# Linear attention into a routed MoE: q transposed as it was loaded, Exp and max on one PSUM bank each, another order of loads

## The chip, the cores and the metric

One core of a Trainium2 chip runs the whole program. The metric is the device time of one execution in microseconds, as the median of several runs. The engines are TensorE (PE, with its weight loads as PEld), VectorE (DVE), ScalarE (ACT), GpSimd (POOL) and SyncE (SP). Loads that change the type on the way (fp32 in memory, fp16 on the chip) are issued by POOL, which puts them all in one queue (q0 in the profile); SP issues plain copies in another (q1).

## The reference

```python
def phi(x):
    return np.where(x > 0, x, np.exp(x) - 1.0) + 1.0
q_p, k_p = (phi(q), phi(k))                      # 8 batches, 8 heads, 576 tokens, 64 wide
kv  = np.einsum('bhsd,bhse->bhde', k_p, v)
z   = np.sum(k_p, axis=2)
num = np.einsum('bhsd,bhde->bhse', q_p, kv)
den = np.einsum('bhsd,bhd->bhs', q_p, z)[..., None] + 1e-06
x   = (num / den)                                # -> (4608, 512)
P = np.exp(x @ w_gate - max)                     # 8 experts
for _ in range(8):                               # Sinkhorn
    P /= P.sum(1, keepdims=True) + 1e-09
    P /= P.sum(0, keepdims=True) + 1e-09
    P *= N / E
for e in range(E):                               # w1: 512 x 1024, w2: 1024 x 512
    out += P[:, e:e + 1] * (np.maximum(x @ w1[e], 0.0) @ w2[e])
```

phi is computed as min(exp(x), max(x + 1, 1)), which is the same function: one Exp on ACT, one add-and-max on DVE, one min on DVE.

## The kernel before

The program has two parts that overlap. The **front** (about the first 125 us) is the attention. It goes in 16 steps, `att(b, g)`, one for each batch and each half of the heads; the text calls them step 0 to step 15 (n = 2b + g). While the steps go on, PE already does the first two matrix products of expert 0 for those groups of 512 tokens whose attention is complete: `layer1` (x times w1 into the banks `hq`, line L717) and a plain second layer (h times w2 into `ye`, L1017). Group 0 needs steps 0 and 1 and expert 0's w1, then its w2; group 1 needs steps 0 to 3 as well; and so on. After the front come the remaining groups of expert 0 and the seven other experts, in a Strassen-like form (L832, L1133).

Order of work. Nothing is scheduled by a compiler. A planner written in the kernel (`_Plan`) holds every task with an engine, a cost in microseconds, dependencies, the pools of buffers it takes, and due times (`after`); it emits tasks in the order of its own list schedule. For the front that order is not searched at build time: the string `_FRONT` lists task numbers with a letter for the engine, some 2200 of them, and the planner follows it. Every engine then executes its own list strictly in that order, so one task that waits holds all behind it on the same engine.

What an attention step does, by the lines of the profile:

- Three loads of 576 KB in memory each: k stays fp32 (`kin`), v and q become fp16 (`vv`, and a slice of `hb` for q). In step 0, k and q are both loaded as fp32 by SP; all other loads are POOL's (L406), which waits where the buffer (3 for k, 3 for v, 3 for q) or one of 8 slots in its queue is not free yet.
- k: Exp (`ek`, L417), add-and-max (`t`, L421), min (L425). kv and z: 36 small matmuls (`kv_ps`, L446), copied to `kvz` by ACT (L359) or DVE (L361).
- q: Exp (`eq`, L477) and add-and-max (`tq`, L480) from the loaded tile in SBUF, min (L484), then 36 transposes on PE (L469) into the two PSUM banks of `att`, then one copy to SBUF (`qpT`, L361 on DVE, L359 on ACT).
- Two halves of 288 columns: den matmuls into both `att` banks (L504), Ln (`rden`, L516), then one Exp for both halves (L521) which gives 1/den; num matmuls into `num_ps`, which shares the one pair of banks of `kv_ps` (L504), and the product with 1/den into xT (L531).

The banks of `att` serve the transposes, both den halves and the routing logits (L548), so these follow one another. Before real work is ready PE runs matmuls on zeros (`yw`, L621), 46 of them. Expert 0's w1 comes in two pieces of 512 columns, w2 in two pieces (L335). A step's v can be loaded only when the step three places before it in that buffer has done its kv matmuls. A tiny POOL copy (`gate`, L437) waits for the last step's v to land.

`sinkhorn` (eight rounds on DVE with a tiny matmul in each) runs after the last logits, beside the second part of expert 0.

Of the kernel before, what the change touches and what calls it, by code (L numbers as in the profile page):

```python
# [141 lines left out]
1n 2p 3p 4p 5p 48s 49m 6p 7p 8p 0g 9p 10p 11p 12p 13p 14p 15p 16p 17p 18p 19p 20p 21p  # L142
22p 23p 54a 50s 51m 60n 61a 114g 115m 120a 24p 25p 55d 56d 62d 63d 26p 27p 52g 53m 64p 65d 57n 58p
121d 59a 28p 29p 75g 76m 77g 78m 82d 122d 30p 31p 66p 32p 33p 79g 80m 34p 116g 117m 35p 36p 37p 38p
39p 81a 87n 83d 89d 84n 67a 68p 40p 88a 90d 69a 70a 41p 85p 86d 91p 92d 42p 43p 73p 93p 44p 45p
74d 71p 126n 128d 104n 127a 118g 119m 94a 105g 106m 72d 46p 95p 96a 47p 129d 97a 123n 109n 124p 125d 130p 143g
144m 153n 579n 154a 131d 98p 99d 580p 141g 142m 581p 132p 133a 147a 100p 101d 582p 583p 584p 586p 588p 587a 148d 155d
585a 590p 107g 108m 145g 146m 134p 135a 589d 156d 149d 150n 592p 593a 594p 136a 170g 171m 180n 151p 152a 110g 111m 112g
113m 157p 158d 596p 139p 591a 140d 182d 159p 595a 160a 181a 598p 183d 168g 169m 172g 173m 137p 138d 161p 162a 597a 599a
197g 198m 195g 196m 175d 600p 602p 184p 185d 603p 610a 174a 176d 207n 616n 177n 601p 608a 163a 606p 607p 199g 200m 224g  # L150
225m 226g 227m 178p 179a 186p 187a 166p 167d 201a 208a 604p 236n 164p 209d 165d 202d 203d 210d 204n 188p 605p 617p 618a
619p 620d 621p 189a 190a 622a 211p 238d 253g 254m 212d 205p 230a 206a 228g 229m 251g 252m 280g 281m 102g 103m 282g 283m
231d 623p 625p 624d 626d 213p 193p 194d 237a 239d 232d 214a 627p 614a 628a 629p 215p 216a 217a 191p 192d 631p 649n 632a
233n 612d 240p 241d 234p 235a 255g 256m 637p 218p 242p 243a 635p 244p 630d 258d 257a 245a 219d 220p 259d 260n 284g 285m
263n 265d 221d 292n 334g 335m 293a 264a 287d 638p 636p 222p 643a 223a 650p 651a 652p 266d 645d 267p 246a 653a 311g 312m
309g 310m 307g 308m 261p 268d 314d 262d 286a 654p 656p 657a 655d 294d 319n 336g 337m 633p 269p 295d 249p 250d 658p 660p
659d 288d 321d 320a 270a 313a 639p 661a 247p 271p 272a 273a 315d 248d 662p 289n 340a 663a 296p 297d 290p 291d 322d 640p
361g 362m 338g 339m 274p 298p 275d 299a 365g 366m 634p 535d 300p 301a 276p 277d 367a 664p 536d 665d 316n 682n 317p 323p
318a 647a 302a 341d 363g 364m 392g 393m 390g 391m 542d 368d 324d 683p 684a 685p 342d 686a 346n 348d 347a 668p 278p 279a
373n 374a 543d 375d 687p 688a 303p 444g 445m 325p 326a 369d 537d 304d 689p 453s 376d 544d 349d 690a 641a 669p 305p 327p  # L160
328a 329a 691p 306d 343n 350p 692d 351d 344p 345a 446g 447m 454s 476g 477m 402n 396a 666p 330p 394g 395m 417g 418m 352p
353a 448g 449m 455s 404d 667p 397d 354p 403a 355a 331d 332p 474g 475m 483s 674a 356a 484s 370n 693p 333d 371p 372d 377p
378d 459n 405d 478g 479m 485s 419g 420m 695p 359p 379p 694a 538s 539m 360d 676d 398d 424d 461d 696a 380a 423a 460a 670p
671p 672p 357p 381p 382a 673p 697p 486g 358d 425d 462d 480a 406p 407d 698d 715n 399n 400p 429n 383a 680a 401a 481d 716p
717a 421g 422m 386p 408p 409a 545s 546m 431d 387d 718p 720p 719a 563d 564d 565d 566s 567m 430a 432d 410p 411a 384p 385d
678a 426n 482d 705p 547s 548m 706p 713a 721a 412a 433p 434d 427p 428d 549d 722p 435p 413p 724p 414d 436a 723a 550d 725d
437p 438a 439a 415p 416d 726p 463p 464a 556d 440p 557d 551d 540s 541m 490n 491a 552s 553m 492d 441d 451d 493d 558d 559s
560m 570g 554s 555m 487n 571n 572g 573m 574g 575m 701p 702p 388p 488p 450a 452d 389a 489a 494p 442p 443d 728p 709d 729d
456n 457p 495a 496p 497a 458d 703p 498p 499a 500a 501p 704p 727d 465p 466a 502d 711d 730p 731a 734p 467p 468a 469a 503p
504d 759d 760d 735p 742a 699p 472p 473d 700p 470p 471d 533n 755d 748d 981s 982m 983s 984m 749d 808d 750d 756d 561s 562m  # L170
707a 751s 752m 985s 986m 987s 988m 757d 758d 753s 754m 738p 739p 732p 763n 733p 534p 809d 810d 761d 811s 812m 813s 814m
989s 990m 991s 992m 505p 506a 740a 508d 507n 576n 577g 578m 764p 778p 765a 766p 767a 780p 781a 770p 771a 768p 769a 772p
736p 774p 993s 994m 779a 784p 785a 782p 783a 746a 773d 775d 509p 510d 786p 787d 788p 789d 776p 737p 973d 815n 777a 816p
817a 511d 790p 791a 818p 819a 822p 820p 744d 762d 821a 823a 830p 832p 833a 831a 824p 825d 794p 826p 866d 867d 827d 834p
836p 837a 838p 795p 840p 974d 868d 839d 869s 870m 828p 829a 512p 835a 841d 513d 802d 792p 793p 874p 875a 800a 876p 877a
1023s 1024m 1025s 1026m 568s 569m 1027s 1028m 842p 880p 798p 514d 924d 878p 843a 844d 881a 975d 925d 845d 926d 846d 515p 796p
799p 797p 804a 871s 872m 927s 928m 516d 929s 930m 873n 884p 882p 885d 883d 888p 848p 517d 879a 889a 894p 976d 886p 895a
849a 890p 891a 806a 898p 892p 893a 847d 899d 854p 887a 896p 518p 850p 851a 855a 519d 520d 897d 852p 900p 932p 901a 853a
858p 859d 856p 857d 946p 933a 938p 902d 903d 904d 939a 521p 934p 522d 860p 935a 861a 936p 942p 906p 948p 931n 937a 943d
947a 944p 952p 949a 940p 953a 523d 941d 908p 954p 955d 945a 950p 956p 907a 951a 995p 996a 909a 957d 524p 525d 526d 997p  # L180
958p 998a 1001p 1002a 912p 1003p 1004d 999p 1005p 1006d 959a 913a 916p 917d 910p 527p 905d 528d 529d 1007p 1009p 1011p 1000a 1010a
1012a 918p 1015p 1016a 1008a 1017p 1013p 1014a 1018d 1019p 919a 530p 531d 532d 712a 1020d 1037p 914p 1039p 1038a 613a 972n 1029s 1030m
1031s 1032m 1033s 1034m 1035s 1036m 1485n 1040a 977d 915d 960p 1021p 1043p 1119s 1120m 1121s 1122m 1123s 1124m 1486g 1487m 1488g 1489m 961p
968d 978d 1044a 1022a 1093d 962p 963p 969a 964p 864a 1045p 966p 1094d 979d 1041p 1095d 1046d 1042a 609a 1047p 611d 681a 965p 1048d
1049p 675d 1051p 1053p 648a 1052a 615d 980d 1054a 1050a 967p 1057p 1058a 1059p 1055p 1061p 1065p 1067p 1096d 971d 1062d 1060d 970d 1063p
1056a 1066a 1071p 1068a 911d 1073p 1069p 1097p 1099p 1100d 679d 1064a 1072a 1101d 1098a 1102p 1103a 1075p 1107p 1110p 1076d 1077p 1079p 1108d
1070a 743d 1111d 1109d 646a 1081p 1113p 1078a 1080a 1085p 1125s 1126m 1127s 1128m 1082a 1087p 1086a 1105a 714a 1104g 1106g 1129s 1130m 1083p
1074d 1089p 1133p 1135p 1084a 1114d 1112d 1088d 1115d 1116p 1090d 1091p 1131s 1132m 1241s 1242m 1243s 1244m 1245s 1246m 1490n 1491g 1492m 1134a
1139p 1136a 642a 1092a 1141p 1140a 1137p 1118d 1117d 1161d 1162d 1165p 1167p 1166a 1170p 1143p 1175p 1138a 644a 1163d 1164d 1169d 710d 1168d
1173a 1174g 1171a 1144d 1178p 1145p 1146a 1147p 1177d 1176d 708d 1172g 1148a 1149p 1150a 1181p 1153p 1179d 1142d 1154a 1155p 1151p 1157p 1183d  # L190
1180d 1182d 1158d 1187p 677a 1189p 1184p 1159p 1215d 1216d 1186d 747d 1185d 1217d 741d 1218d 1152a 1188a 1193p 801a 1190a 1195p 1191p 1219p
1221p 1194a 1222d 1196d 1223d 1192a 1220a 1224p 1227a 1228g 923a 1160a 1197p 1198d 1156d 1229p 1231d 1232p 1230d 1493d 865d 1233d 1199p 1200a
1201p 1202a 1203p 1204a 803a 1235p 1207p 1209p 1247s 1248m 1205p 1208a 1211p 1225a 1236d 1494d 1495d 1237d 1249s 1250m 1251s 1252m 1253s 1254m
1255p 1363s 1364m 1365s 1366m 1257p 1238p 1212d 1206a 1256a 1210d 1213p 1261p 1258a 1263p 1259p 1367s 1368m 1214a 807a 1240d 1234d 1239d 1287p
1262a 1288a 1283d 1289p 1292p 1284d 1285d 1293a 1291d 1290d 1286d 1265p 1297p 1300p 745d 1266d 1267p 1260a 1299d 1302d 1298d 1301d 1269p 1271p
1303p 1268a 1270a 1275p 1264d 1272a 1277p 1273p 1304d 1337d 1305d 1276a 1279p 1309p 1311p 1306p 1338d 1274a 1226g 1280d 1281p 1295a 1310a 863a
# [41 lines left out]
def kernel(  # L238
# [17 lines left out]
    P = 128  # L256
# [1092 lines left out]
```

## Time and profile before

| | us |
|---|---|
| median of 3 runs | 951.93 (951.27 to 953.01) |
| the profiled execution, whole | 951.94 |
| its span (first to last instruction) | 950.1 |
| PE busy in the span | 939.9 (99%) |
| DVE / ACT / POOL busy | 765.3 / 575.8 / 144.3 |
| 16 DMA engines, mean busy share 0 to 30, 30 to 60, 60 to 95 us | 1.07, 1.14, 0.89 |

The profiled execution takes 1.84 us more than its span, and is as long as the median. A share of DMA engines of about 1 or more means that all 16 had packets in flight all the time. In the rows below a line begins with its start in us; "idle before" is how long the engine had stood still and what ended that. A landing time in the text is the start of an issue plus the time from issue to landing that the trace gives for this one issue.

### The profile page before, as it was taken

To read this page: it belongs to the slowest core of one execution; us is meant where nothing else is said; L and a number is where in the kernel's file an instruction comes from. 1 tells how busy PE (TensorE), PEld (TensorE's weight loads), DVE (VectorE), ACT (ScalarE), POOL (GpSimd) and SP (SyncE) were. 2 spreads that over 40 slices of the span, in tenths; PEclk is the share of its full clock that TensorE was granted. 3 is DMA by queue.
4 is the path that set the end of the run, shared out by engine and by line. 5 is a ranking of instruction groups with operands and counts; after the bars stand their busy time and mean duration, and the time that the engine had idled before them with its cause. 6 is when DMAs were issued, how large, how long until landed. Compare 5 with 4: busy or idle time off the path is not lost.

```text
span 950.1 us, 19908 instructions
## 1 busy us (share of the span) xinstructions
PE 939.9 (99%) x7816; PEld 631.7 (66%) x7816; DVE 765.3 (81%) x1479; ACT 575.8 (61%) x1025; POOL 144.3 (15%) x204
## 2 busy tenths in 40 slices
PE   9999999999999999999999999999999999999997
PEld 4444478666676666766677666766667666776665
DVE  7699899879877888788887888878887888877776
ACT  6899856666655555555555555555555555555552
POOL 5433100011111111110011111111112111111110
PEclk9999999999999999999999999999999999999999
DMA  9989793452254222652236222652226422215544
GB/s 239 265 185 235 170 230 94 122 122 78 79 126 86 75 77 78 162 122 78 79 87 119 79 78 78 152 114 70 68 67 143 111 78 78 73 45 166 167 134 134
DMA packets 82042, 112.75 MB, mean 119 GB/s; under 512 B 7324, under 2 KB 46236, under 8 KB 81948
## 3 DMA queue, kind: packets, MB, share of 16 engines
q1 hardware_dynamic: 56876, 75.59, 26.0%
q0 software_dynamic: 24320, 34.78, 19.6%
q8 instruction: 61, 1.00, 0.4%
q10 hardware_dynamic: 752, 1.11, 0.3%
q14 instruction: 33, 0.27, 0.1%
HBM read 119.69 MB, written 17.69 MB: 145 GB/s over the span
## 4 chain that ended last, share of the span: by engine, by line
PE 94%; DMA 4%; ACT 1%; DVE 1%; POOL 0%; issue 0%
PE ye L1133 35%; PE hq L832 24%; PE R L832 12%; PE Zye L832 6%; PE Zye L1133 6%; PE ye L1017 5%; PE hq L717 3%; DMA w<-in_moe_w_dram 2%; DMA vv<-in_v_dram 2%; PE kv_ps L446 1%; PE att L504 0%; PE num_ps L504 0%; PE hq L1229 0%; DMA kin<-in_k_dram 0%; PE att L469 0%; PE R L1229 0%
## 5 line engine op out<-in xcount | busy, mean ns | idle before, releaser
L1164 DVE SCALAR_TENSOR_TENSOR acc<-ye,P_sb,acc 128x256 f32<-128x256 f32 x620 | 268.4, 479 | 126.9 <-PE ye L1133 126.2
L1133 PEld LDWEIGHTS <-S 128*128 128x128 f16 x1984 | 194.0, 98 | 46.6 <-DVE S L1104 0.2
L1133 PE MATMUL ye<-T,S 128*128 128x256 f16 x1488 | 192.8, 273 | 0.0
L1174 POOL TENSOR_TENSOR acc<-acc,st 128x256 f32<-128x256 f32 x124 | 88.1, 730 | 635.2 <-ACT st L1171 624.0
L832 PEld LDWEIGHTS <-W 128*128 128x128 f16 x1248 | 122.1, 98 | 86.6
L1133 PEld LDWEIGHTS <-hb 128*128 128x128 f16 x1536 | 150.3, 98 | 42.5 <-issue 1.3
L863 ACT ACTIVATE hb<-hq 128x512 f16<-128x512 f32 x134 | 80.2, 598 | 136.6 <-PE hq L832 130.2
L832 PE MATMUL R<-xs,W 128*128 128x512 f16 (+1 forms) x560 | 150.0, 358 | 0.0
L832 PE MATMUL hq<-xs,W 128*128 128x512 f16 (+1 forms) x560 | 150.0, 358 | 0.0
L832 PE MATMUL hq<-xs,w 128*128 128x512 f16 (+1 forms) x560 | 139.7, 358 | 0.0
L832 PEld LDWEIGHTS <-w 128*128 128x128 f16 x936 | 91.5, 98 | 59.8 <-issue 0.5
L860 ACT ACTIVATE hb<-Zye 128x512 f16<-128x512 f32 x134 | 80.1, 598 | 38.5 <-PE Zye L832 38.3
L1171 ACT ACTIVATE st<-Zye,P_sb 128x256 f32<-128x256 f32 x124 | 52.5, 471 | 77.2 <-PE Zye L1133 77.0
L866 DVE CUSTOM_DVE_ANT_0 hb<-hq,sx 128x512 f16<-128x512 f32 x126 | 86.6, 687 | 15.0 <-PE hq L832 14.9
L853 ACT COPY sx<-hq 128x512 f32<-128x512 f32 x126 | 73.6, 584 | 35.3 <-PE hq L832 35.3
L849 ACT COPY Zye<-hq 128x512 f32<-128x512 f32 x134 | 77.9, 581 | 22.6 <-PE hq L832 22.4
L866 DVE CUSTOM_DVE_ANT_0 hb<-R,sx 128x512 f16<-128x512 f32 x126 | 86.5, 687 | 4.9 <-ACT sx L853 3.8
L1104 DVE TENSOR_TENSOR S<-hb 128x1024 f16<-128x1024 f16 x124 | 85.0, 686 | 5.0 <-ACT hb L863 5.0
L832 PE MATMUL Zye<-xs,w 128*128 128x512 f16 (+1 forms) x280 | 75.0, 358 | 0.0
L857 ACT COPY sx<-R 128x512 f32<-128x512 f32 x126 | 74.4, 591 | 0.0
L1133 PE MATMUL ye<-w,hb 128*128 128x256 f16 x512 | 66.3, 273 | 0.6 <-DVE acc L1164 0.5
L1133 PE MATMUL Zye<-w,hb 128*128 128x256 f16 x512 | 66.3, 273 | 0.0
(119 smaller groups left out, 940.8 us busy)
## 6 DMA issues: line engine op xcount, KB each, us to landing
xs<-xd SPq DMA_DIRECT2D x196, 256.0 KB, 3.3
w<-in_moe_w_dram POOLq DMA_DIRECT2D x18, 512.0 KB, 7.7
kin<-in_k_dram POOLq DMA_DIRECT2D x15, 576.0 KB, 7.4
out_dram<-acc SPq DMA_DIRECT2D x61, 128.0 KB, 2.4
w<-in_moe_w_dram POOLq DMA_DIRECT2D x7, 1024.0 KB, 9.8
xs<-xd SPq DMA_DIRECT2D x49, 128.0 KB, 3.2
vv<-in_v_dram POOLq DMA_DIRECT2D x16, 288.0 KB, 7.2
hb<-in_q_dram POOLq DMA_DIRECT2D x15, 288.0 KB, 6.4
```

Source lines behind the costliest of these rows:

```text
L832: nc.tensor.matmul(dst_[:, p, :] if parts == 2 else dst_.rearrange("p a b -> p (a b)"), lhsT=lhs(p, c), rhs=blk[i](c), start=(first and p ...
L849: nc.scalar.copy(out=Zt[1], in_=gX["tile"])
L853: nc.scalar.copy(out=gs2["tile"], in_=gX["tile"])
L857: nc.scalar.copy(out=gs5["tile"], in_=gR["tile"])
L860: nc.scalar.activation(out=dst(0, 0), in_=Zt[1], func=AF.Relu)
L863: nc.scalar.activation(out=dst(1, 0), in_=gX["tile"], func=AF.Relu)
L866: nc.vector._custom_dve(TENSOR_ADD_SAT, out=out_, in0=ps, in1=sb, s0=3.0e38, s1=0.0)
L1104: nc.vector.tensor_tensor(out=Sx[:, i], in0=a0, in1=a1, op=op)
L1133: nc.tensor.matmul(bank(g_)[:, s, :], lhsT=lhs(s, kk), rhs=rhs(kk), start=(new and s == 0 and kk == 0), stop=(kk == 3), skip_group_check=True)
L1164: nc.vector.scalar_tensor_tensor(out=dst(), in0=bank(g_)[:, s, :], scalar=P_sb[:, gg, e:e + 1], in1=dst(), op0=ALU.mult, op1=ALU.add)
L1171: nc.scalar.mul(out=gst["tile"], in_=bank(g_)[:, s, :], mul=P_sb[:, gg, e:e + 1])
L1174: nc.gpsimd.tensor_tensor(out=dst(), in0=dst(), in1=gst["tile"], op=ALU.add)
```

## The change

Five things change together.

1. From step 1 on, q is transposed straight from the loaded fp16 tile. Exp and add-and-max then read PSUM: ACT takes one of the two banks and DVE the other, then they swap. The min works in SBUF on the transposed tile, so `tq` and the copy to `qpT` are gone. In step 1 the banks are `ye0` and `ye1` in place of `att`. Step 0 stays as it was.
2. In steps 0 and 1 the Exp that gives 1/den is done by halves, each as soon as its Ln is done.
3. POOL issues in another order. Before: k of step 1, v0, k2, q1, v1, q2, v2, first half of w1, q3, k3, second half of w1, v3, q4, w2 in two pieces, and so on, with the identity built ahead of all. Now: v0, k1, q1, the identity, v1, w1 columns 0 to 255, q2, w1 columns 256 to 511, w1 columns 512 to 1023, k2, q3, v2, k3, v3, w2 in two pieces, q4, k4, k5, q5, the gate's weights, v4, v5, and so on.
4. `_FRONT` is new as a whole, with other costs and due times. On PE the zero matmuls are 38 in place of 46, 28 of them ahead of step 0's transposes in place of 26. All other PE instructions keep their kind and number.
5. In `sinkhorn` the scaled matrix is written in its plain layout and the sum over tokens reads it with a stride; before, the write had the stride.

```diff
 _FRONT = """
...
+            ts_.append(add(("dma", costs[len(ts_)] if costs else 2.6), lambda _: None, deps=[ti],
+                           use=[g, *gsw], prio=prio, lat=2.65 if costs and len(ts_) != 1 else 1.95))
+        return g, ts_ if costs else [ts_[0], ts_[-1]]
...
+            return load_w(moe_w1, "w1", p_w1, [[((slice(None), slice(None), slice(a, a + n)),
+                                                 a, [[F, P], [P * F, NDT], [1, n]])] for a, n in ((0, 256), (256, 256), (512, 512))],
+                          e, shape=[P, NDT, F], costs=(1.33, 1.33, 2.6), **kw)
...
-        ga = [S_.grp(p_att), S_.grp(p_att)]
+        ga = [S_.grp(p_ye[0]), S_.grp(p_ye[1])] if n == 1 else [S_.grp(p_att), S_.grp(p_att)]
...
-                        nc.tensor.transpose(qps()[half(r), hh, j, :], gtq["tile"][half(hh), j, r, :],
+                        nc.tensor.transpose(qin(hh)[half(r), j, :],
+                                            gtq["tile"][half(hh), j, r, :] if n == 0 else gin["q"]["tile"][half(hh), r, j, :],
                                             ident[half(hh), half(hh)])
...
-        t2 = fadd(("act", 1.16), f_qe, deps=[t0], use=[gin["q"], geq], prio=pr)
-        t3 = fadd(("dve", 0.455 if n else 0.77), f_qm, deps=[t0], use=[gin["q"], gtq], prio=pr)
-        tm = fadd(("dve", 0.76), f_qp, deps=[t2, t3], use=[geq, gtq], prio=pr)
-        t1 = fadd(("pe", 0.29), f_qt, deps=[tm, t_id[0]], acq=ga, use=[gtq], prio=pr, cfg=1)
-        tq = fadd({"act": 1.13, "dve": 0.76 if b < NR else 1.24}, f_qc, deps=[t1], acq=[gq], use=[*ga, gq], prio=pr)
...
+            t1 = fadd(("pe", 0.29), f_qt, deps=[tin["q"], t_id[0]], acq=ga, use=[gin["q"]], prio=pr, cfg=1)
...
+            for hs in range(2):
+                def f_qe(_, hs=hs):
+                    o, i = qio(geq["tile"], hs)
+                    nc.scalar.activation(out=o, in_=i, func=AF.Exp)
+
+                def f_qm(_, hs=hs):
+                    o, i = qio(gq["tile"], hs)
+                    nc.vector.tensor_scalar(out=o, in0=i, scalar1=1.0, scalar2=1.0, op0=ALU.add, op1=ALU.max)
+                pair = []
+                for dve in (hs, 1 - hs):
+                    pair.append(fadd(("dve", 0.46 if b < NR else 0.7) if dve else ("act", 0.6), f_qm if dve else f_qe,
+                                     deps=[ta if dve else t0, *pair], use=[ga[hs], gq if dve else geq], prio=pr))
+                te2 += pair
+
+            def f_qp(_):
+                nc.vector.tensor_tensor(out=gq["tile"], in0=gq["tile"], in1=geq["tile"].rearrange("p r j d -> p r (j d)"), op=ALU.min)
+            tq = fadd(("dve", 0.76), f_qp, deps=te2, use=[geq, gq], prio=pr)
...
-        te_ = fadd(("act", 1.18), f_ex, deps=tl, use=[grd], prio=pr)
+            if n < 2:
+                te_.append(fadd(("act", 0.62), f_exh, deps=[tl[c]], use=[grd], prio=pr))
+            elif c == 0:
+                te_ = [fadd(("act", 1.18), f_ex, deps=tl, use=[grd], prio=pr)] * 2
...
-                nc.vector.tensor_tensor(out=wc.rearrange("p e g -> p g e"), in0=P0_sb,
+                nc.vector.tensor_tensor(out=wt, in0=P0_sb,
                                         in1=Rr[:, :, None].broadcast_to([P, NTT, E]), op=ALU.mult)
-                nc.vector.tensor_reduce(gs, wc, AXX.X, ALU.add)
+                nc.vector.tensor_reduce(gs, wt.rearrange("p g e -> p e g"), AXX.X, ALU.add)
...
-    for i in range(46):
-        twa = add(("pe", 0.43 if i < 9 else 0.215), f_warm, deps=[twa], use=[gyw], prio=900.0, after=1.2 + 0.25 * i)
+    for i in range(38):
+        twa = add(("pe", 0.43 if i < 14 else 0.215), f_warm, deps=[twa], use=[gyw], prio=900.0, after=1.2 + 0.25 * i)
```

More of the change, by code (lines that the diff above doesn't have):

```diff
@@ L147 @@
[L147 to L156, printed above, removed]
@@ L323, with load_w @@
     p_sw = S_.pool(8)
-    def load_w(ten, nm, pl, pieces, e, prio, deps=(), shape=None):
+    def load_w(ten, nm, pl, pieces, e, prio, deps=(), shape=None, costs=None):
         g = S_.grp(pl)
@@ L370 @@
     v_land, all_land, kv_id, t_id = [], [], [], [None]
+    first_ld = {"sp": None, "pool": None, "w": None}
     def fadd(*a, **kw):
@@ L459, in att, with qin @@
         gq, geq = S_.grp(p_qpT), S_.grp(p_eq)
-        ga = [S_.grp(p_att), S_.grp(p_att)]
+        ga = [S_.grp(p_ye[0]), S_.grp(p_ye[1])] if n == 1 else [S_.grp(p_att), S_.grp(p_att)]
         def qps():
             return at2.bitcast(FP16)[:, :, 0:S].rearrange("p h (j w) -> p h j w", w=PW)
+        def qin(hh):
+            if n == 1:
+                return ga[hh]["tile"].bitcast(FP16)[:, 0:S].rearrange("p (j w) -> p j w", w=PW)
+            return qps()[:, hh]
         def f_qt(_):
+            for hh in range(2 if n == 1 else 0):
+                ga[hh]["tile"] = yps.tile([P, 512], FP32, tag=f"ye{hh}", name=f"ye{hh}")
             for j in range(NJ):
@@ L473, in f_qa @@
             geq["tile"] = fp.tile([P, 2, NJ, D], FP16, tag="ek", name="eq", bufs=3)
-            gtq["tile"] = fp.tile([P, NJ, 2, D], FP16, tag="tq", name="tq")
-        def f_qe(_):
-            nc.scalar.activation(out=geq["tile"], in_=gin["q"]["tile"], func=AF.Exp)
-        def f_qm(_):
-            nc.vector.tensor_scalar(out=gtq["tile"].rearrange("p j r d -> p r j d"), in0=gin["q"]["tile"], scalar1=1.0, scalar2=1.0, op0=ALU.add, op1=ALU.max)
-        def f_qp(_):
-            tv = gtq["tile"].rearrange("p j r d -> p r j d")
-            nc.vector.tensor_tensor(out=tv, in0=tv, in1=geq["tile"], op=ALU.min)
@@ L495, in att @@
[L495 to L498 removed]
+            if n == 0:
+                gtq["tile"] = fp.tile([P, NJ, 2, D], FP16, tag="tq", name="tq", bufs=1)
@@ new lines, in f_gq, with qio, f_qe, f_qm @@
+        def f_gq(_):
+            gq["tile"] = fp.tile([P, 2, S], FP16, tag="qpT", name="qpT")
+        def qio(t, hs):
+            dst = t.rearrange("p r j d -> p r (j d)") if len(t.shape) == 4 else t
+            if n > 1 and b >= NR:
+                return dst[:, hs].rearrange("p (w j) -> p w j", j=NJ), qin(hs).rearrange("p j w -> p w j")
+            return dst[:, hs], qin(hs).rearrange("p j w -> p (j w)")
+        gtq = S_.grp(p_tq)
+        if n == 0:
+            def f_qe(_):
+                nc.scalar.activation(out=geq["tile"], in_=gin["q"]["tile"], func=AF.Exp)
+            def f_qm(_):
+                nc.vector.tensor_scalar(out=gtq["tile"].rearrange("p j r d -> p r j d"), in0=gin["q"]["tile"], scalar1=1.0, scalar2=1.0, op0=ALU.add, op1=ALU.max)
+            def f_qp(_):
+                tv = gtq["tile"].rearrange("p j r d -> p r j d")
+                nc.vector.tensor_tensor(out=tv, in0=tv, in1=geq["tile"], op=ALU.min)
+            def f_qc(e):
+                f_gq(e)
+                copy(e, gq["tile"], at2.bitcast(FP16)[:, :, 0:S])
+            t0 = fadd(("none", 0.0), f_qa, deps=[tin["q"]], acq=[gtq, geq], prio=pr)
+            t2 = fadd(("act", 1.16), f_qe, deps=[t0], use=[gin["q"], geq], prio=pr)
+            t3 = fadd(("dve", 0.77), f_qm, deps=[t0], use=[gin["q"], gtq], prio=pr)
+            tm = fadd(("dve", 0.76), f_qp, deps=[t2, t3], use=[geq, gtq], prio=pr)
+            t1 = fadd(("pe", 0.29), f_qt, deps=[tm, t_id[0]], acq=ga, use=[gtq], prio=pr, cfg=1)
+            tq = fadd({"act": 1.13, "dve": 0.76}, f_qc, deps=[t1], acq=[gq], use=[*ga, gq], prio=pr)
+        else:
+            t1 = fadd(("pe", 0.29), f_qt, deps=[tin["q"], t_id[0]], acq=ga, use=[gin["q"]], prio=pr, cfg=1)
+            t0 = fadd(("none", 0.0), f_qa, deps=[t1], acq=[geq], prio=pr)
+            ta = fadd(("none", 0.0), f_gq, deps=[t1], acq=[gq], prio=pr)
+            te2 = []
+            for hs in range(2):
[10 more added lines that the diff above has]
+                te2 += pair
+            def f_qp(_):
+                nc.vector.tensor_tensor(out=gq["tile"], in0=gq["tile"], in1=geq["tile"].rearrange("p r j d -> p r (j d)"), op=ALU.min)
+            tq = fadd(("dve", 0.76), f_qp, deps=te2, use=[geq, gq], prio=pr)
@@ L499, in att @@
+        tqs = [tq]
         grd = S_.grp(p_rden)
@@ L521, in f_ex, with f_exh @@
             nc.scalar.activation(out=grd["tile"], in_=grd["tile"], func=AF.Exp, scale=-1.0)
-        te_ = fadd(("act", 1.18), f_ex, deps=tl, use=[grd], prio=pr)
+        te_ = []
+        for c in range(2):
+            def f_exh(_, c=c):
+                nc.scalar.activation(out=grd["tile"][:, c], in_=grd["tile"][:, c], func=AF.Exp, scale=-1.0)
+            if n < 2:
+                te_.append(fadd(("act", 0.62), f_exh, deps=[tl[c]], use=[grd], prio=pr))
+            elif c == 0:
+                te_ = [fadd(("act", 1.18), f_ex, deps=tl, use=[grd], prio=pr)] * 2
         for c in range(2):
@@ L598, in f_d @@
                 nc.vector.reciprocal(cc, Dc)
-            a = add(("dve", 2.29 if it == 0 else 2.78), f_a, deps=last, prio=-200.0)
+            a = add(("dve", 2.07 if it == 0 else 2.56), f_a, deps=last, prio=-200.0)
             c = add(("pe", 0.112), f_c, deps=[a, t_apsx], acq=[gc], prio=-200.0, lat=0.1)
@@ L636 @@
     gsw = S_.grp(p_sw)
-    ti = add(("pool", 0.8), f_wg, acq=[gsw], use=[gsw], prio=-96.5, after=1.75)
+    ti = add(("pool", 0.8), f_wg, acq=[gsw], use=[gsw], prio=-96.5, after=1.75, deps=[first_ld["pool"]])
     wg_done.append(add(("dma", 0.3), lambda _: None, deps=[ti], use=[gsw], prio=-96.5, lat=2.15))
```

204 lines of the change are left out of this document (103 added, 101 removed).

## The prediction

> **What bounds the kernel now.** I read the page first: share of each engine, then the chain that ended last.
>
> ```profile
> PE 939.9 (99%) x7816; PEld 631.7 (66%) x7816; DVE 765.3 (81%) x1479; ACT 575.8 (61%) x1025; POOL 144.3 (15%) x204
> PE 94%; DMA 4%; ACT 1%; DVE 1%; POOL 0%; issue 0%
> ```
>
> TensorE is the bound, and the change takes no real matmul away. So time can come only from moments in which PE does nothing useful: the start, and holes. The table by 5 us (stretch:its end, then busy us of PE, PEld, DVE, ACT, POOL with counts, clock, DMA share, GB/s) shows where the holes are:
>
> ```profile
> 25.00:30.00 5.00, 4.44 (x98) 2.18 (x95) 2.41 (x5) 4.18 (x9) 2.17 (x3) 1.00 1.23 206
> 30.00:35.00 5.00, 4.32 (x61) 1.93 (x60) 2.38 (x4) 3.28 (x5) 1.10 (x2) 1.00 1.18 268
> 35.00:40.00 5.00, 4.52 (x61) 2.02 (x59) 2.72 (x4) 4.37 (x7) 1.77 (x3) 1.00 1.15 297
> 95.00:100.00 5.00, 4.03 (x76) 1.78 (x77) 4.75 (x9) 4.58 (x8) 0.00 (x0) 1.00 0.98 210
> ```
>
> Until 40 us the DMA engines are full and PE is not; from 40 to 95 PE has no hole; one follows at 99. PE's timeline names them:
>
> ```profile
> 1.33 8.58 PE L621 MATMUL yw<-hb 128*128 128x512 f16 x26 [1.33 <-DVE hb L611]
> 9.84 0.48 PE L469 MATMUL att<-ident,tq 64*64 64x64 f16 x36
> 20.60 1.04 PE L717 MATMUL hq<-xT,w 128*128 128x512 f16 x4
> 25.66 1.90 PE L717 MATMUL hq<-xT,w 128*128 128x512 f16 x8 [0.56 <-DMA w<-in_moe_w_dram]
> 34.09 3.61 PE L1017 MATMUL ye<-w,hb 128*128 128x512 f16 x16 [0.68 <-DMA w<-in_moe_w_dram]
> 38.82 0.32 PE L504 MATMUL att<-qpT,kvz 64*64 64x288 f16 x4 [0.48 <-ACT kvz L359]
> 99.75 0.70 PE L446 MATMUL kv_ps<-vv,t 64*64 64x128 f16 x36 [0.97 <-DMA vv<-in_v_dram]
> 108.29 0.48 PE L469 MATMUL att<-ident,tq 64*64 64x64 f16 x36 [0.32 <-ACT P_sb L552]
> ```
>
> And the chain of waits over the first 40 us confirms what stands behind 34.09:
>
> ```profile
> 18.00 16.05 DMA w<-in_moe_w_dram
> 34.05 0.04 issue
> 34.09 3.61 PE ye L1017 x16
> ```
>
> The second half of w2 was issued at 18.00 and landed at 34.1, behind a full queue. That is the gate of the front: 24 of group 0's 32 second-layer matmuls need it.
>
> **The loads.** Issue start plus time to landing, in the queue's order: q3 21.65, k3 23.05, w1's second half 25.63, v3 27.09, q4 28.53, w2 31.01 and 34.10. A 576 KB load thus takes 1.40 to 1.46 (I use 1.44), a w1 half 2.5. POOL issues far ahead (10 to 16 us to landing), so landings go by bytes alone. In the new order the same loads precede w2's end but one, q4: 34.10 - 1.44 = **32.66**, with w2's first half at 29.6, v3 at 27.1, all of w1 at about 19.9 (w1 stood behind eleven loads at 25.63, now behind seven). The two w1 pieces of 256 columns have rows of half the size: their price is between 0 and 1.3 us each (as slow as a whole half). The gate's weights land 0.2 us after the load ahead of them, in 512 rows of 32 bytes, so a row costs little by itself; I take 0.
>
> **Ahead of the gate.** 28 zero matmuls end at 1.33 + 8.58 + 2 x 0.214 = 10.3 instead of 9.9, so step 0's transposes start 0.5 later. v0, k1, q1, v1 land at about 8.2, 9.6, 11.1, 12.6 (q1 and v1 before: 13.14 and 14.75), and q of step 1 goes to PE at once. Following the lists by hand with the rows' durations, I get the first L717 at about 17.3 instead of 20.6, and 28 of the 32 first-layer matmuls by about 24 instead of 29.4. Then PE is short of data, waiting for v2, v3, and w2 at 29.6. Step 3 runs from v3: kv at 27.9, its first den at 29.1, Ln by 30.9, the num of its first half at 32.0. That is 0.7 before w2's end, so w2 stays the gate, and the early start is only cover: nothing of the 3.3 us shows at the end. The identity, now behind three POOL issues of 0.72 to 0.86, is ready near 4 and needed at 10.3. Being 0.7 late with kv of step 3 would cost nothing; each us beyond is paid in full.
>
> At the gate both have done the same 32 and 8 matmuls. New: step 3's first num (0.15) is done as well, step 4's transposes (0.35) are not. Lead: 34.09 - 32.66 - 0.20 = **1.2 us**.
>
> **After the gate.** Before, PE stood 0.65 longer than its work from 37.65 to 38.82 (1.17, against 0.52 for 36 kv matmuls elsewhere). New, 8 + 8 second-layer and 8 first-layer matmuls and the logits stand between, and v4 (about 40.0, PE there at 41.4) has landed: **+0.65**. Later, 99.75: its v load could be issued only at 93.31, after kv at 92.30 had freed the buffer, and landed at 99.7, 6.8 after that kv's end. The new list has 7.5 us of work at that place (12 matmuls 2.69, 8 for 1.83, 8 for 1.83, small ones 1.2): **+1.07**. At 108.29 the transposes waited for the `att` bank, whose logits lay in ACT's queue behind an Exp of k, with one kv (0.52) as cover; 0.50 lost; two of the three later logits now have four matmuls (0.97) as cover, but the first is again followed by a kv and transposes: **+0.5**. Against this I set **0.8** for holes the new list will have (0.3 at that first logits, 0.5 elsewhere).
>
> **DVE and ACT** must keep up, or PE waits; from 60 to 95 us they are busy 32.9 and 33.4 of 35.
> - DVE, of 15 steps: gone are 13 copies net at 0.757 and 15 L480 at 0.477 (17.0). New are 30 add-and-max of 576 from PSUM. No row shows one. Nearest: the fp16 copy of 1152 out of PSUM at 0.757, less half its length at 0.52 ns an element, 0.457; upper end 0.754, the L531 row of 576 fp32. I take 0.457, for type and memory are the same: 13.7. Four more evacuations add 2.5. Net -0.8.
> - ACT: Exp of 576 from PSUM, between 0.598 (relu of 512) and 0.738 (Ln of 576); the rows for 256 and 512 (0.370, 0.589) extended give 0.644, taken. 30 x 0.644 - 15 x 1.162 = +1.9; four half Exp for two whole ones +0.4; two 1.11 copies and four evacuations gone, -4.4. Net -2.1.
> - Sinkhorn: the strided write takes 0.675, a plain one (L577) 0.453; 8 x 0.22 = 1.8 of DVE gained, or nothing if the strided read costs as much. It lies beside a PE that is 100% busy from 125 to 170.
>
> None of these is on the path; they are cover for the lead. The Trainium skill, VectorE: DVE Perf Modes, "Why PSUM operands drop a tier", speaks against this edit: an operand in PSUM caps the add-and-max at half the speed it has from fp16 in SBUF. By its table of cycles a half would be 0.43 us (an estimate), and the sum stays as it is; it rules out the upper end, which the trace of before cannot.
>
> **Sum.** 1.2 + 0.65 + 1.07 + 0.5 - 0.8 = 2.6 us. On the profiled span 950.1 - 2.6 = 947.5, plus the 1.84 outside it 949.3; that execution (951.94) is as long as the median, so **949.3**. A change under 0.2% (1.9 us) can't be told from none.
>
> **Rivals.**
> 1. *The gate does not move* (17%). The half-size w1 rows cost 0.6 each, or step 3 comes 1.2 late. Against it: DMA share above 1.1 throughout. Lead gone: 1.4 gained, 950.5.
> 2. *The `att` banks become the wait* (10%). A step held them 0.35 + 0.1 + 0.757 for the q part; the swap makes it 0.35 + two halves of 0.65 + 0.15, 0.6 more. Between steps 4 and 15 (32.93 to 108.29) a step has 6.9 us and its den halves need some 2, so only halves that wait behind a 1.16 us Exp in ACT's queue make it tight. Six such steps of 0.4 on PE: 951.7.
> 3. *Slower: DVE becomes the bound* (8%). Place: 35 to 108 us, 24 add-and-max. At 0.754 each they cost 7.1 us more than I take; DVE's slack there is 2.1 in 35 us, 4.4 in all, plus the 0.8, of which the lead itself uses 2.6. Some 4.5 us fall on PE: 953.8. It decides from about 0.57 us each.
> 4. *PE runs cold while it waits* (4%). The first 14 zero matmuls are 0.428 us apart, later ones 0.214, so PE has a slow state after rest and needs about 6 us to leave it: 14 x 0.214 = 3.0 us, 952.3. Between 24 and 32.7 PE has about 5.6 us of work and no gap over 1.5. The Trainium skill, TensorE: Matmul & The Clock Gate, "Why this matters for your kernels", warns of idle gaps beyond about 3 us; no gap before is that long.
> 5. *w2 comes earlier still* (3%), its last half in 2.5 instead of 3.09: 948.7, and 947.9 without new holes.
>
> My forecast has the rest, 58%, with its own range 948.0 to 950.0 (holes between 0.2 and 2). Range for 8 in 10: rivals 1 and 2 belong in it, and the nearer half of 3: 947.8 to 953.0. Faster by over 0.2% (below 950.0): 0.58 + 0.03 and the nearer part of rival 1, 0.62. Within: the rest of 1, and 2 and 4, 0.26. Slower: rival 3 and the bad end of 2, 0.12.
>
> **What would show it.** w2's second half landing near 32.7 and the L1068 row (L1017 now) right behind it; first L768 (L717 now) near 17.3; PE idle between 24 and 32; no hole near 99 and 108; add-and-max of 576 near 0.46, Exp of 576 near 0.64. I am wrong if w2 lands after 33.5, if PE's rows after 35 us name `att` or DVE as what ended their idle time for over 2 us in all, or if add-and-max takes over 0.57.

## The result, and the profile after

The changed kernel takes 968.3 us (median of 4 runs, 967.9 to 969.1), the kernel before 951.6 beside it (4 runs, 950.7 to 953.0): a ratio of 1.0175, 95% interval 1.0158 to 1.0193. It is 16.7 us slower, where 2.6 us faster was forecast. The profiled execution has a span of 966.4 us.

The page's first line and the chain that ended last hardly tell where 16 us went:

```profile
PE 944.7 (98%) x7808; PEld 634.1 (66%) x7808; DVE 767.0 (79%) x1485; ACT 575.0 (59%) x1036; POOL 144.2 (15%) x205
PE 90%; DVE 4%; ACT 3%; DMA 2%; issue 1%; DVEq 0%; ACTq 0%
```

PE's share fell by one point and those of DVE and ACT by two; but in the chain ACT and DVE together went from 2% to 7%. The table by 10 us (busy us of PE, PEld, DVE, ACT, POOL, then the granted clock, DMA share, GB/s) shows the places:

```profile
50.00:60.00 10.00, 9.06 (x194) 4.56 (x194) 7.41 (x12) 8.04 (x12) 2.22 (x4) 1.00 0.68 171
100.00:110.00 10.00, 8.30 (x191) 4.02 (x189) 8.96 (x19) 7.44 (x12) 0.00 (x0) 1.00 0.52 122
110.00:120.00 10.00, 7.30 (x85) 2.98 (x75) 5.68 (x11) 5.71 (x10) 0.00 (x0) 0.80 0.46 134
120.00:130.00 10.00, 9.23 (x118) 4.22 (x117) 7.44 (x13) 7.45 (x12) 0.77 (x2) 0.86 0.35 107
150.00:160.00 10.00, 7.53 (x43) 4.87 (x42) 9.07 (x23) 3.22 (x7) 0.00 (x0) 0.83 0.66 184
```

The kernel before had, in three of these stretches:

```profile
50.00:60.00 10.00, 10.00 (x226) 5.34 (x224) 8.32 (x13) 9.24 (x15) 2.87 (x4) 1.00 1.07 238
110.00:120.00 10.00, 10.00 (x103) 4.04 (x92) 7.15 (x12) 6.79 (x10) 2.44 (x4) 1.00 0.79 163
150.00:160.00 10.00, 10.00 (x95) 9.00 (x94) 9.65 (x21) 6.97 (x14) 0.00 (x0) 1.00 0.06 16
```

PE was 100% busy in most of them. DVE and ACT are not fuller than before but emptier (but for ACT from 120 to 130 us), so neither has become the bound: they wait for one another, and PE for them. PE's timeline first confirms the start, and then shows the damage:

```profile
16.40 1.04 PE L768 MATMUL hq<-xT,w 128*128 128x512 f16 x4
32.41 1.90 PE L1068 MATMUL ye<-w,hb 128*128 128x512 f16 x8
40.97 0.70 PE L453 MATMUL kv_ps<-vv,t 64*64 64x128 f16 x36
114.21 1.04 PE L600 MATMUL att<-wg_sb,xT 128*128 128x8 f16 x36 [2.16 <-DVE qpT L533]
117.31 1.89 PE L768 MATMUL hq<-xT,w 128*128 128x512 f16 x4
119.75 1.89 PE L1068 MATMUL ye<-w,hb 128*128 128x512 f16 x4
153.08 0.60 PE L883 MATMUL R<-sx,W 128*128 128x256 f16 x4 [2.47 <-DVE hb L917]
154.56 1.06 PE L883 MATMUL hq<-sx,w 128*128 128x256 f16 x4
```

Until 41 us the rows come near their forecast times, and w2's second half is used at 32.41 in place of 34.09. Then come holes that name `att` and `qpT`. About 2 us behind the hole of 2.16 us, after a second one of 0.54, four matmuls take 1.89 us instead of 1.04, and behind the one of 2.47 four of half the size take 1.06 instead of 0.60. In stretches of 2 us the granted clock is 0.50 to 0.51 from 116 to 122 us and 0.50 from 154 to 156. The Trainium skill, TensorE: Matmul & The Clock Gate, "Why this matters for your kernels", names gaps beyond some 3 us as the danger; here the clock fell behind gaps of 2.2 and 2.5 us, and in the run whole_banks below it stayed at 1.00 behind one of 3.24, so the length of one gap does not decide it.

The list of what PE waited for (20 to 175 us: in total, times, longest) has a new kind of entry; these are four of its rows:

```profile
PE att L600 <- DVE qpT L533: 3.2, 2, 2.2
PE R L883 <- DVE hb L917: 2.5, 1, 2.5
PE att L549 <- DVE qpT L541: 2.2, 4, 0.8
PE att L549 <- ACT eq L529: 1.7, 1, 1.7
```

What stands behind it is seen in one step. These are the rows of step 6's q part up to its first den matmul, in which Exp is L529, add-and-max L533 and the min L541 (rows of other work between them are left out):

```profile
52.02 0.65 ACT L529 ACTIVATE eq<-att 128x576 f16<-128x576 f16 x1
52.70 0.46 DVE L533 TENSOR_SCALAR qpT<-att 128x576 f16<-128x576 f16 x1 [0.86 <-ACT eq L529]
53.19 0.65 ACT L529 ACTIVATE eq<-att 128x576 f16<-128x576 f16 x1 [0.53 <-DVE qpT L533]
53.88 0.46 DVE L533 TENSOR_SCALAR qpT<-att 128x576 f16<-128x576 f16 x1 [0.72 <-ACT eq L529]
54.37 0.76 DVE L541 TENSOR_TENSOR qpT<-qpT,eq 128x1152 f16<-128x1152 f16 x1
55.18 0.32 PE L549 MATMUL att<-qpT,kvz 64*64 64x288 f16 x4 [0.76 <-ACT rden L566]
```

The two engines do not work on one bank each and swap. They take turns: Exp, max, Exp, max. The q part takes 54.37 - 52.02 = 2.35 us ahead of the min, where the prediction had 1.45. (The profile puts PE's 0.76 us down to `rden`, which ended at 55.17; the min that the den matmul reads ended at 55.13.) In step 1, whose banks are `ye0` and `ye1`, the same pieces overlap a little: the first add-and-max starts 0.11 us before the first Exp has ended, and the second Exp 0.14 us before the second add-and-max has:

```profile
11.50 0.65 ACT L529 ACTIVATE eq<-ye 128x576 f16<-128x576 f16 x1
12.04 0.81 DVE L533 TENSOR_SCALAR qpT<-ye 128x576 f16<-128x576 f16 x2
...
12.71 0.64 ACT L529 ACTIVATE eq<-ye 128x576 f16<-128x576 f16 x1
```

The difference between the two steps: `ye0` and `ye1` are two tiles, `att` is one tile of two banks. In the built program the add-and-max on the second bank of `att` carries a semaphore wait for the Exp on its first bank, although they share no bank; on `ye0` and `ye1` it waits for the transposes only.

### The profile page after: what moved, and what is told of

Read it like the earlier page. It is cut to its first block, busy times and chain, and to the rows that moved or that the text cites. A ratio compares the mean times of both kernels' runs of the same rounds, so it can differ in the third digit from the quotient of the medians.

```text
span 966.4 us, 19875 instructions
## 1 busy us (share of the span) xinstructions
PE 944.7 (98%) x7808; PEld 634.1 (66%) x7808; DVE 767.0 (79%) x1485; ACT 575.0 (59%) x1036; POOL 144.2 (15%) x205
## 4 chain that ended last, share of the span: by engine, by line
PE 90%; DVE 4%; ACT 3%; DMA 2%; issue 1%; DVEq 0%; ACTq 0%
PE ye L1184 35%; PE hq L883 23%; PE R L883 12%; PE Zye L883 6%; PE Zye L1184 6%; PE ye L1068 3%; PE hq L768 2%; DMA w<-in_moe_w_dram 2%; ACT eq L529 1%; PE yw L672 1%; DVE qpT L533 1%; PE att L549 1%; DVE qpT L541 1%; PE num_ps L549 0%; ACT rden L561 0%
## 5 line engine op out<-in xcount | busy, mean ns | idle before, releaser
L917 DVE CUSTOM_DVE_ANT_0 hb<-hq,sx 128x512 f16<-128x512 f32 x126 | 86.4, 686 | 15.1 <-PE hq L883 14.9
```

Source lines behind the costliest of these rows:

```text
L917: nc.vector._custom_dve(TENSOR_ADD_SAT, out=out_, in0=ps, in1=sb, s0=3.0e38, s1=0.0)
```

## The experiments

Theory A: the turns on the one `att` tile are the cause. Theory B: the new loads and the new front order are late. Theory C: reading PSUM loads ACT and DVE too much. The table has all runs; the kernel before had medians of 951.8 to 951.9 beside them.

| run | median us | ratio to before (95%) |
|---|---|---|
| the changed kernel | 968.3 | 1.0175 (1.0158 to 1.0193) |
| two_tiles | 958.9 | 1.0074 (1.0057 to 1.0091) |
| whole_banks | 964.4 | 1.0141 (1.0122 to 1.0159) |
| before_two_tiles | 953.5 | 1.0017 (1.0008 to 1.0026) |
| weights_early | 965.1 | 1.0146 (1.0130 to 1.0163) |
| two_tiles_w_early | 963.8 | 1.0126 (1.0109 to 1.0143) |
| two_tiles_w1first | 951.4 | 1.0002 (0.9990 to 1.0013) |
| after_w1first | 964.0 | 1.0130 (1.0116 to 1.0144) |
| before_w2first | 951.9 | 1.0001 (0.9992 to 1.0010) |
| w1first_q4early | 953.2 | 1.0017 (1.0007 to 1.0027) |
| two_tiles_w_fill, w1first_fill | 963.6, 951.2 | 1.0126 (1.0107 to 1.0145), 0.9997 (0.9988 to 1.0005) |

### Two tiles for the two banks

```diff
-    at2 = aps.tile([P, 2, 512], FP32, tag="att", name="att")
+    atb = [aps.tile([P, 512], FP32, tag=f"at{i}", name=f"att{i}") for i in range(2)]
...
-                nc.scalar.activation(out=grd["tile"][:, c], in_=at2[:, :, 0:CH], func=AF.Ln, bias=eps_t)
+                for r in range(2):
+                    nc.scalar.activation(out=grd["tile"][:, c, r], in_=atb[r][:, 0:CH], func=AF.Ln, bias=eps_t)
```

> The changed kernel with its two att banks as two tiles, and Ln done bank by bank (two of about 0.40 us in place of one of 0.74, 32 more ACT instructions); the order of every engine is kept. Theory A (one tile of two banks makes Exp and max take turns, so a step's q part holds the banks 2.3 us instead of about 1.3, PE waits for it from 50 us on, and the cold clock and the late weights of expert 1 follow from the lateness): L529 and L533 overlap, PE's idle time from 50 to 165 us falls from 12 us to under 3, clock 1.00 throughout, 949.5 us (947.5 to 953). Theory B (the new order of loads and of the front is what is late): no more than 3 us come back, 965 or more. Theory C (reading PSUM, and the load on ACT and DVE): 968 or more, since ACT gets 2 us more to do.

958.9 us: 9.4 of the 16.7 us came back. That is clear of theories B and C, but above the range given for A: PE's idle time from 50 to 160 us fell from 12.2 to 4.0 us and not under 3, and the clock was 0.83 from 140 to 150 us. Step 6 in this run's timeline (Exp is L530, add-and-max L534, min L542):

```profile
52.53 1.26 ACT L530 ACTIVATE eq<-att 128x576 f16<-128x576 f16 x2
52.64 1.03 DVE L534 TENSOR_SCALAR qpT<-att 128x576 f16<-128x576 f16 x2 [0.56 <-PE att L483]
53.82 0.76 DVE L542 TENSOR_TENSOR qpT<-qpT,eq 128x1152 f16<-128x1152 f16 x1
```

Both engines now work without a pause, and the q part takes 1.29 us. Neither is slower than in turns (between 30 and 100 us a max takes 0.454 us on average, 0.456 in the changed kernel, an Exp 0.654 and 0.649), so it was the wait and not the chip that kept them apart; that fits the Trainium skill, PSUM — Partial Sum Buffer, "PSUM bank collisions raise a hardware error", by which two engines may use different banks at the same time. PE's list of waits for 20 to 175 us is down to this:

```profile
PE R L885 <- DVE hb L919: 3.1, 1, 3.1
PE att L550 <- ACT rden L563: 0.9, 1, 0.9
PE num_ps L550 <- DVE kvz L364: 0.5, 1, 0.5
PE att L550 <- DVE kvz L364: 0.3, 1, 0.3
PE att L483 <- ACT rden L563: 0.2, 1, 0.2
```

No wait for `qpT` or `eq` is left. B and C fall for that part, since loads, order and engine work are the same (ACT has more). One hole stands, at 141.6 us, and it is not the swap's.

### One handover instead of three

```diff
+                    if n > 1 and hs == 1:
+                        return
+                    sl = slice(0, 2) if n > 1 else hs
-                    o, i = qio(geq["tile"], hs)
+                    o, i = qio(geq["tile"], sl)
                     nc.scalar.activation(out=o, in_=i, func=AF.Exp)
```

The add-and-max likewise: from step 2 on each is one instruction over both banks.

> The changed kernel, but from step 2 on ACT does Exp over both banks at once (1.16 us) and DVE then add-and-max over both (about 0.76): one handover instead of three. Theory A: the turns are what costs; a step's q part takes 1.16 + 0.76 + two waits of about 0.1 instead of 0.65 + 0.46 + 0.65 + 0.46 + four waits, so 2.1 instead of 2.5 us, and a part of the loss comes back: 962 to 966. Theory B: 967 to 969. Theory C: about 966, from 0.3 us less of engine time in each step.

964.4, within theory A's range; theory C's 966 is not excluded by this run alone (962.9 to 966.2). Its step 6 has Exp at 53.56 for 1.13 us, max at 54.72 and the min at 55.51: 1.95 us, 0.40 less. Not all of the 3.9 us gained can be put down to that. PE's idle time from 50 to 130 us is 7.9 us after 9.7, so 1.8 are fewer waits. The clock differs too: in the profiled execution it is 1.00 from 40 us on, and the four executions take from 962.9 us at a mean clock of 0.998 to 966.2 at 0.994, which is the mean clock of the changed kernel (0.993 to 0.995). The clock stays up although PE has its longest gap here:

```profile
150.31 0.60 PE L891 MATMUL R<-sx,W 128*128 128x256 f16 x4 [3.24 <-DVE hb L925]
```

Doing both banks one after the other, without any swap, was better than the swap as built.

### Control: the kernel before with two tiles

> The kernel before, with its att banks as two tiles, Ln by banks and the qpT copy as two copies of 576: a control for the first run. The kernel before has no step where ACT and DVE use the two banks at once, so theory A expects no gain: 951.0 to 952.5. If two tiles are good in themselves (logits and halves come free sooner): below 950.5.

953.5, ratio 1.0017 (1.0008 to 1.0026): not a gain, but a cost of some 1.7 us, which I had not expected. Splitting Ln and the qpT copy is not free even where PE is the bound; which of the two costs, and where, was not tried. The run with two tiles pays for its Ln too, but not for the copy, which the change took out from step 1 on. In ACT's groups between 30 and 100 us a Ln of 288 columns takes 0.510 us and one of 576 takes 0.741; but the second of a pair starts before the first has ended, so a pair fills 0.89 us of ACT's timeline, 0.15 more than one long Ln:

```profile
51.08 0.89 ACT L563 ACTIVATE rden<-att,eps_t 128x288 f32<-128x288 f32 x2
```

### The last hole: expert 1's weights

In the changed kernel the last hole begins with DVE, whose combination of expert 1's weights waits, with PE's `hb` behind it in DVE's list:

```profile
146.18 0.69 DVE L1110 TENSOR_TENSOR W<-w 128x1024 f16<-128x1024 f16 x1 [3.06 <-DMA w<-in_moe_w_dram]
```

POOL issues these weights after a small memset of acc6, which waits until the stores out of acc6 are done (127.72 us here, 113.14 before). The first idea was lateness: let the memset write another buffer.

```diff
-        nc.gpsimd.memset(acc[NA - 1][:, 0:4:2, 0:4], 0.0)
+        nc.gpsimd.memset(gate, 0.0)
```

> The changed kernel, only the small POOL memset after which expert 1's weights are issued writes another buffer, so that it does not wait for the stores out of acc6. Theory A with a separate last part: the weights are issued some 30 us earlier, the 3.06 us wait of the combination L1110 and PE's 2.47 us at 150 us go, and with them the slow clock of 150 to 158 us: 963.5 to 965, while the waits from 50 to 125 us stay as they are. If that hole only hid another one (the combinations are late in any case, because DVE is behind): 967 to 969.

965.1, near what was expected: the wait at 146 us is gone. But the same edit on top of two tiles went the wrong way:

> The run with two tiles, and the POOL memset writes another buffer, so that expert 1's weights are issued near 98 us (w2 still first). No wait for them in either theory of the run above: PE's 3.15 us and about 2 us of slow clock go, 952 to 954.5. If what the prediction summed for the loads and the front (2.6 us) is real, it shows against the control with two tiles (953.5): 950.5 to 952; if not, 953.5 or more.

963.8, 4.9 us more than without it. My expectation was wrong. With the weights issued from 92.15 us on, DVE's timeline has this instead:

```profile
103.71 0.43 DVE L815 TENSOR_TENSOR acc<-xT 128x512 f16<-128x512 f16 x1 [4.95 <-DMA xd<-acc]
112.34 0.42 DVE L815 TENSOR_TENSOR acc<-xT 128x512 f16<-128x512 f16 x1 [6.87 <-DMA xd<-acc]
```

and PE's timeline the holes that follow from it:

```profile
105.53 0.46 PE L550 MATMUL num_ps<-qpT,kvz 64*64 64x288 f16 x4 [4.93 <-DVE xT L585]
113.82 0.47 PE L453 MATMUL kv_ps<-vv,t 64*64 64x128 f16 x9 [5.15 <-DVE xT L585]
```

The weights share the DMA engines with the stores out of acc6 (DMA share 1.13 from 100 to 110 us, 0.59 in the run with two tiles), DVE needs acc6 again, and the products into xT stand behind that in its list. SP issued two of these stores from 94.86 us on, 2.7 us behind the first of the weights, and they took 8.8 and 17.1 us to land, against a median of 4.5 in the run with two tiles. In weights_early the order was the other way round, the stores from 97.50 us on and the weights from 98.60, and DVE waited for them only 1.3 us. The memset that looks like a needless wait keeps the weights out of the way of those stores.

The other suspect is the order. After the memset the changed kernel issues w2 of expert 1 first and then the two halves of w1; the kernel before has w1 first. w2 is as large as both halves of w1. So only POOL's three issues were exchanged, by changing places in `_FRONT`:

```diff
-603g 604m
+598g 599m
...
-598g 599m
+600g 601m
...
-600g 601m
+603g 604m
```

> The run with two tiles, and POOL issues expert 1's w1 ahead of its w2, as the kernel before does (the changed kernel has w2 first); PE, DVE, ACT and SP keep their lists. If that order is what makes DVE's combination W wait 3.74 us for w1 at 134.7 us: no wait there, PE's 3.15 us at 141.6 us and the slow clock behind it (about 2 us) go, 953 to 955 us after 958.9. If it is the late issue (118.4 us, 113.6 in the kernel before): the wait shrinks but another on w2 stays, 956.5 to 959.

951.4, below the 953 to 955 expected: the order it was. POOL's timeline of this run:

```profile
116.48 0.10 POOL L1304 MEMSET acc<- 128x8 f32 x1 [24.55 <-DMA xd<-acc]
116.92 1.43 POOL L336 DMA_DIRECT2D w<-in_moe_w_dram  x2 [0.35 <-issue]
118.99 0.91 POOL L336 DMA_DIRECT2D w<-in_moe_w_dram  x1 [0.64 <-issue]
```

The memset is hardly earlier than in the run with two tiles (116.78), but w1's halves land 6.5 us after their issue (median), where they needed 13.5 behind w2. DVE's combination at 130.5 us waits for nothing, and the clock is 1.00 throughout. The median fell by 7.5 us, more than the 5.1 by which the two profiled spans differ; the profiled execution with two tiles (956.3) was the shortest of its four.

> The changed kernel, only POOL issues expert 1's w1 ahead of its w2 (att stays one tile). If the order is a loss of its own, beside the turns of Exp and max: DVE's 3.06 us wait for w1 at 146 us and PE's 2.47 us with the slow clock behind it (about 1.8) go, and the waits from 50 to 125 us stay: 963.0 to 965. If the late issue (129.3 us) matters beside the order: 965.5 to 968.

964.0, so the order is worth 4.3 us with the turns left in, and the turns 964.0 - 951.4 = 12.6 with the order mended. Alone the two give 9.4 + 4.3 = 13.7, together 16.9. So 3.2 us come only of both at once; that late steps and late weights lengthen one another would explain it, but was not shown.

> The kernel before, only POOL issues expert 1's w2 ahead of its w1, as the changed kernel does. w1 would land near 113.6 + 14 = 127.6 us, and DVE's first combination of it (L1059) comes at 130.7 us: if the order hurts only together with lateness and the four combinations in a row of the new DVE list, nothing changes, 951.4 to 952.4. If the order costs by itself: 954 or more.

951.9, no change. Here the issue comes early enough: w2 goes out at 113.62 us, the halves of w1 land at about 128 and 131 (issues at 115.21 and 115.9, 12.8 and 15.1 to landing), and DVE's first combination starts at 131.14 without a wait. In the run with two tiles DVE wants the same weights at nearly the same time, 134.74 - 3.74 = 131.0, but w2 goes out only at 118.39. So w2 first does harm together with the late issue. The kernel before also has the four combinations of expert 1 spread from 130.7 to 151.1 us with PE's `hb` between them, where the changed kernel has them in a row; no run shows what that is worth by itself.

### The gate of the front by itself

In the last kernel q of step 4 is issued ahead of w2 again, as before the change; the lists of PE, DVE, ACT and SP are the same.

```diff
+172g 173m
 108g 109m
...
-172g 173m
```

> The run with two tiles and w1 first, only POOL issues q of step 4 ahead of expert 0's w2, as the kernel before does. This takes back the largest step of the prediction by itself. If w2's end is the gate of the front: the second half of w2 lands 1.4 us later, PE's L1070 row at 32.4 us moves to about 33.8 with a DMA wait, and 1.2 to 1.4 us are lost: 952.4 to 953.2 after 951.4. If something else sets that place (the prediction's first rival): 0 to 0.4 us.

953.2, so 1.8 us are lost. w2's second half lands at 19.37 + 13.5 = 32.9 instead of 17.30 + 14.2 = 31.5, which is 1.4 later. PE's timeline shows a wait, but not where it was expected: it is at w2's first half, while PE comes to the second at 34.34, when that has landed:

```profile
30.31 1.86 PE L1070 MATMUL ye<-w,hb 128*128 128x512 f16 x4 [1.26 <-DMA w<-in_moe_w_dram]
...
34.34 1.90 PE L1070 MATMUL ye<-w,hb 128*128 128x512 f16 x8
```

The four matmuls behind the wait take 1.86 us, 1.04 in the kernel with the new order, and the clock is 0.83 from 30 to 40 us. So the 1.8 us are not the landing alone. The one execution of eleven with a mean clock of 1.000 took 951.7 us, and the five such of the kernel with the new order took 951.0 to 951.4: by these few, some 0.5 us are left to the landing, and the rest comes with the slow clock, which this kernel has more often (a mean clock of 0.998 or less in ten of eleven executions, against four of eleven).

### PE kept busy in the holes between 25 and 29 us

Five zero matmuls were put into PE's two holes there.

```diff
                 heads(atb, c, 1)
+                if n == 2 and c == 0:
+                    fill(3)
...
                                          start=(j == 0), stop=(j == NJ - 1))
+            if n == 3:
+                fill(2)
```

> The run before this one, with 5 zero matmuls of 512 columns on PE in its holes between 25 and 29 us (3 after the first den half of step 2, 2 after the kv of step 3), into ye0, which is free there. In the run with two tiles those holes were 0.86 and 0.53 us and the clock fell to 0.51 to 0.64 from 28 to 32 us; the matmuls behind w2's second half began 0.46 us later than in the changed kernel. If a slow clock after holes costs time at the gate: clock 1.00 there and 0.3 to 0.6 us less than the run before this one. If not: the same within 0.2, or 0.2 more.

> The run with two tiles and w1 first, with the 5 zero matmuls in PE's holes between 25 and 29 us. If some executions lose time to a slow clock after those holes: the spread (951.0 to 955.2 in the run without) shrinks and the median falls by 0.2 to 0.6. If not: the same within 0.2.

963.6 after 963.8, and 951.2 (950.6 to 954.0) after 951.4 (951.0 to 955.2): nothing that can be told from no change. In the run with two tiles the clock did fall to 0.51 to 0.64 from 28 to 32 us, but in the profiled executions of the two kernels compared here it was 1.00 without the filling too, with holes as long, so the experiment did not meet the case it was made for. Whether filling the holes would keep the clock up stays open.

No kernel beats the one before by an amount that can be measured; the last one, at 0.9997 (0.9988 to 1.0005), is level with it.

## Why the prediction was wrong

- **Ahead of the gate: right in size, wrong in the wait.** Step 0's transposes began at 10.16 (10.3 forecast), the first L768 at 16.40 (17.3), and PE stood between 25 and 29 us. By the prediction's own sum the lead is 34.09 - 32.41 - 0.20 = 1.5 us, where the term had 1.2. But "so w2 stays the gate" did not come true: w2's second half landed at 31.4 (32.66 forecast), and PE used it 1.0 us later without a wait. The waits that set the place are those of steps 2 and 3, whose first num for step 3 came at 32.16, as forecast (32.0):

```profile
26.64 0.32 PE L549 MATMUL att<-qpT,kvz 64*64 64x288 f16 x4 [1.22 <-DVE kvz L364]
27.80 0.32 PE L549 MATMUL att<-qpT,kvz 64*64 64x288 f16 x4 [0.84 <-ACT rden L561]
29.39 0.32 PE L549 MATMUL num_ps<-qpT,kvz 64*64 64x288 f16 x4 [0.53 <-DVE kvz L364]
```
- **The holes at 38 and 99: right.** The kv of step 4 runs without a wait at 40.97, and no later row waits for `vv`. In the table of 10 us the kernel with two tiles and w1 first has 9.76 and 10.00 us of PE in 30 to 40 and 90 to 100, where the kernel before has 8.84 and 9.03.
- **The hole at 108: wrong.** The logits that were to have cover are the two that wait most, 1.01 and 2.16 us, for an add-and-max on `att`.
- **The failing step** is the one that put the swap off the path: "The `att` banks become the wait", where the swap "makes it 0.35 + two halves of 0.65 + 0.15". That read the source (ACT on one bank, DVE on the other) and not the waits of the built program. With turns the term is 2.35 and not 1.45, and it does not come in six steps but in all 14 that use `att`. The rival was named, with 10% and six steps of 0.4 us, 2.4 in all; the runs give 9.4 (turns taken out alone) to 12.6 (order mended too). The term of 0.8 us for new holes stands against 9.7: that is PE's idle time from 50 to 130 us (10.00 less its busy time, summed over the eight stretches), and it is 0.85 in the kernel with two tiles and w1 first. The prediction's own sign of being wrong came true: PE's rows after 35 us name `att`'s readers for far more than 2 us (3.2 + 2.2 + 1.7 in the list above).
- **The slow clock** (the fourth rival, 3.0 us at 4%) came, but elsewhere in the profiled execution. Between the spans of the changed kernel and of the one with two tiles and w1 first lie 966.4 - 949.4 = 17.0 us. PE's busy time up to 180 us differs by 175.92 - 163.75 = 12.2. The rest, 4.8, fits the matmuls at the low clock behind the two long holes: by the clock column they lose 10 x (0.20 + 0.14 + 0.17) = 5.1 us. At the place that the rival named it came in the profiled executions of other runs (0.87 from 30 to 40 us in whole_banks, weights_early and after_w1first).
- **Expert 1's weights** were in no term. The change of `_FRONT` put w2 ahead of w1 behind the memset, and the prediction followed the loads up to w2 of expert 0 only.
- **Durations: right but for the last two steps.** Exp of 576 takes 0.650 us (0.644 forecast), add-and-max 0.457 between 40 and 100 us (0.457). In the last two steps, where the kernel writes it into another layout, it takes 0.75, so that the mean of all 28 is 0.498; the prediction had one price for all. DVE is not the bound, and the third rival falls. Sinkhorn gained nothing, the second of the two values given: the plain write is cheaper, the strided sum dearer by as much, 0.458 + 0.673 after 0.675 + 0.453.

```profile
L635 DVE TENSOR_REDUCE gs<-wt 128x8 f32<-128x288 f32 x5 | 3.4, 673 | 0.2
L633 DVE TENSOR_TENSOR wt<-P_sb,Rr 128x288 f32<-128x288 f32 x5 | 2.3, 458 | 0.2
```

- **What is left of the 2.6 us.** With both faults mended the kernel is at 1.0002, and the control that pays for the split Ln and copy is at 1.0017. Against that control the rest of the change brings some 1.4 to 2.1 us at most: the two intervals overlap, and the control also pays for the split copy, which the mended kernel does not have. Whether the swap could run in parallel without splitting Ln was not tried.

## What to carry to other kernels

Before two engines are given a bank each, look in the built program whether they wait for one another: one tile of two banks was kept in order as if it were one bank, and two tiles cost a second Ln but freed 9 us and more. When an order written out by hand is replaced, compare every queue to its end, not only around the change: three exchanged issues at 117 us cost 4 to 7 us. A wait that looks idle may hold back traffic; measure before it is taken away.

## What was not expected of the hardware

- Behind gaps of 2.16 us (with one of 0.54 two us later) and of 2.47 us four matmuls of 512 columns took 1.89 us instead of 1.04, or four of 256 took 1.06 instead of 0.60 (clock 0.50 to 0.51). In whole_banks a gap of 3.24 us left the clock at 1.00. In the run with two tiles, gaps of 0.86 and 0.53 us between 25 and 29 us came before a clock of 0.51 to 0.64; with w1 first, gaps of 0.84 and 0.53 at the same place left it at 1.00. So the same gap comes with and without a slow clock; what decides was not found.
- Two Ln of 288 columns fill 0.89 us of ACT's timeline, one of 576 fills 0.74: the split costs 0.15 us, and not the 0.28 by which the listed durations differ (2 x 0.510 against 0.741).
- A chain off the busy engine's own work was hardly hidden. Ten of the steps (6 to 15) run between 50 and 130 us. There the turns add 1.06 us to a step's q part, and PE's idle time is 9.7 us with them and 0.8 with two tiles: some 0.9 us a step reached PE (an estimate from these two sums).
